# Attention into a SoLU feed-forward layer on one core: a planner that counts TensorE instructions and open transfers, sixteen transposes moved to DMA, constants and first key casts moved off GpSimd

## The chip, the core and the metric

The kernel runs on one core of a Trainium2 chip. The core has five engines, each with an instruction queue of its own: TensorE (PE in the profile, its weight loads PEld), VectorE (DVE), ScalarE (ACT), GpSimd (POOL) and SyncE (SP, which here only issues transfers). Sixteen DMA engines move the data. The metric is the device time of one execution in microseconds (us), lower is better.

## What is computed

Inputs are q, k and v of shape (4 batches, 8 heads, 768 positions, 64), float32, and the feed-forward weights. Each query sees the first 8 positions and the 96 latest ones; a bias grows with the distance. The attention output of all heads is one row of 512 per token (3072 tokens), and each row goes through a SoLU layer with a layer norm and an output product.

```python
scores = scale * np.matmul(q, k.transpose(0, 1, 3, 2)) + bias
scores = np.where(is_global | is_local, scores, -1e9)
a = exp(scores - max); a = a / sum(a)
x = np.matmul(a, v)                      # -> (3072, 512)
h = x @ w_in                             # w_in  512 x 1024
solu = h * softmax(h)
ln = (solu - mean) / sqrt(var + 1e-6) * g_ln
out = ln @ w_out                         # w_out 1024 x 512
```

## The kernel before

The program is built in two passes. First the kernel describes its work as 1,316 steps: each has an engine, a duration in ns, a priority, the steps that it depends on, the buffers that it takes and frees, and a function that records its instructions (`step`, line 146). Then `Plan.order` (line 165) plays the steps through: an engine that is free takes the waiting step of lowest priority number whose buffers are to be had, and the order in which steps start is the order in which their instructions are recorded. Priorities come from the table `PRIO` (line 28), one number for each step, which replaces those written in the code. The instruction order of every queue is therefore fixed when the program is built; on the chip each queue runs it in order and waits on semaphores. Where the planner sees a gap of over 330 ns on TensorE in the first 60 us, it puts in dummy matmuls on `busy16` (line 1187).

The steps, by stage:

- **Constants** (lines 410 to 495): identity matrices, the local bias `bw`, masks and ones, most of them written by GpSimd.
- **Loads**: SyncE issues nearly all (`load`, line 634). q and k of a pair of heads come in one transfer of 384 KB, v in two; for the first 256 positions of batch 0 there are small loads `qnat` and `knat` in the natural layout. The feed-forward weights `w_out` are 4 transfers of 512 KB on SyncE, `w_in` 2 on GpSimd's queue.
- **Per batch and pair of heads**: GpSimd casts q and k to fp16 (line 752), TensorE transposes them (line 765), DVE copies them out of PSUM (lines 775, 777). TensorE adds bias and scores (lines 868, 878), ACT takes the exponential into `eb` (line 886).
- **Per unit of 256 or 384 queries**: scores of the global keys (line 921), sums of the exponentials (lines 946, 953), products with v (lines 1030, 1039); the reciprocal of the sums goes through DRAM (`rd`, `rb`) in batches 1 to 3; DVE multiplies it in and writes `xT` (line 1077).
- **Per token tile** (24 tiles of 128 tokens): TensorE makes h with 8 matmuls of 512 columns (line 1110, here g1), ACT its exponential `ef` (line 1117), DVE the product `uu` (line 1120), ACT the sum of squares (line 1124). TensorE transposes `uu` in 8 pieces (line 1131), DVE copies them to `uT` (line 1135), and 8 more matmuls of 512 columns with the scaled weights `gw_out_sb` give the output (line 1169, here g2). ACT scales it into `osb` (line 1175), and SyncE stores 256 KB (line 1177). The weights `gw_out_sb` are first scaled by ACT (line 680), their mean is taken by 8 matmuls (line 686, here the mean step), and DVE writes the final ones (line 690).

A loaded weight and a matmul are two TensorE instructions, so 8 matmuls are 16 instructions. `uT` has 7 buffers, `uu` 3, `osb` 3. PSUM has 8 banks; g1 takes a pair of them, g2 one, a transposition of `uu` one.

Of the kernel before, what the change touches and what calls it, by code (L numbers as in the profile page):

```python
# [18 lines left out]
P = 128  # L19
# [106 lines left out]
"""  # L126
LDQ = 4


class Plan:  # L130

# [1094 lines left out]
```

## Time and profile before

| | before |
|---|---|
| median of 3 runs | 196.66 us (195.24 to 197.91) |
| the profiled execution | 194.31 us |
| its span from the first to the last instruction | 192.1 us |
| mean granted TensorE clock | 0.952 of full speed |
| bytes moved by DMA | 33.62 MB |

The page of the profile gives the busy time of each engine, the span in 40 slices, the DMA queues, and the chain of waits: the work that ended last, followed back from the end. In the chain "issue" is time in which an engine waited for nothing that the profile shows. The view of waits lists who waited for whom; the view by windows gives for any stretch the busy time of each engine, the number of its instructions and the busy share of the DMA engines; the timeline lists instructions in order of time.

### The profile page before, as it was taken

How to read it: one execution, taken by the hardware profiler on the slowest of the kernel's cores; microseconds unless marked ns; L12 is line 12 of the kernel's file. 1: busy time of each engine (PE TensorE's matmuls, PEld its weight loads, DVE VectorE, ACT ScalarE, POOL GpSimd, SP SyncE). 2: the span in 40 equal slices, each digit the busy share in tenths (PEclk: the TensorE clock that was granted, in tenths of full speed). 3: DMA queues.
4: the chain of work that ended last, by engine and by line, in shares of the span. 5: the costliest groups of instructions: out<-in, count | busy, mean ns of one | idle time of the engine just before them, and what ended most of it. 6: DMA issues, size and time to landing. Idle time of an engine off the chain costs nothing.

```text
span 192.1 us, 5950 instructions
## 1 busy us (share of the span) xinstructions
PE 168.4 (88%) x2456; PEld 98.1 (51%) x2456; DVE 109.6 (57%) x237; ACT 120.4 (63%) x228; POOL 56.9 (30%) x142
## 2 busy tenths in 40 slices
PE   6959779959799979977799999999999289999992
PEld 2434555646355565746445466774656124555550
DVE  1985254855389996544454667774474622555820
ACT  2001967895799865552479993686987002997861
POOL 7889546533260547303513105300000000000000
PEclk9987999996999999997999999999999958999998
DMA  6988985799989297999489997700009900130052
GB/s 142 276 220 158 268 207 125 190 359 372 221 294 307 67 286 224 252 232 306 153 190 195 240 254 214 228 20 0 3 5 218 269 12 0 43 121 3 0 218 109
DMA packets 48363, 33.62 MB, mean 175 GB/s; under 512 B 32417, under 2 KB 43729, under 8 KB 48337
## 3 DMA queue, kind: packets, MB, share of 16 engines
q1 hardware_dynamic: 45536, 31.64, 59.9%
q0 software_dynamic: 544, 1.05, 3.1%
q10 hardware_dynamic: 2256, 0.56, 1.3%
q8 instruction: 19, 0.31, 0.7%
q14 instruction: 8, 0.06, 0.1%
HBM read 27.92 MB, written 6.37 MB: 178 GB/s over the span
## 4 chain that ended last, share of the span: by engine, by line
PE 61%; DVE 11%; issue 11%; ACT 10%; DMA 3%; POOL 1%; ACTq 1%; POOLq 0%; DVEq 0%
PE bank L1169 20%; PE bank L1110 16%; PE bank L1039 5%; PE bank L765 5%; PE bank L1131 4%; ACT ef L1117 3%; ACT eb L886 3%; DVE uu L1120 3%; PE bank L868 2%; DVE gw_out_sb L690 2%; PE bank L878 2%; DMA qnat<-in_q_dram 2%; DVE qT L777 2%; PE bank L1030 2%; DVE uT L1135 2%
## 5 line engine op out<-in xcount | busy, mean ns | idle before, releaser
L1169 PE MATMUL bank<-gw_out_sb,uT 128*128 128x512 f16 x192 | 46.2, 390 | 0.1
L1110 PE MATMUL bank<-w_in_sb,xT 128*128 128x512 f16 x192 | 45.5, 385 | 0.0
L1120 DVE SCALAR_TENSOR_TENSOR uu<-ef,bank 128x1024 f16<-128x1024 f16 x24 | 29.1, 1220 | 28.1 <-ACT ef L1117 28.1
L886 ACT ACTIVATE eb<-bank 128x896 f16<-128x896 f32 (+3 forms) x36 | 29.2, 855 | 21.7 <-PE bank L878 21.5
L1117 ACT ACTIVATE ef<-bank 128x1024 f16<-128x1024 f32 x24 | 24.5, 1021 | 20.2 <-PE bank L1110 20.1
L1169 PEld LDWEIGHTS <-uT 128*128 128x128 f16 x192 | 18.4, 100 | 26.7 <-issue 6.9
L1110 PEld LDWEIGHTS <-xT 128*128 128x128 f16 x192 | 18.2, 100 | 20.8 <-issue 1.6
L1124 ACT ACTIVATE sq<-uu 128x1024 f16<-128x1024 f16 x24 | 25.4, 1059 | 3.5 <-DVE uu L1120 3.0
L1039 PE MATMUL bank<-eb,v 64*64 64x160 f16 (+4 forms) x464 | 18.1, 227 | 9.8 <-issue 9.2
L1175 ACT ACTIVATE osb<-bank,rstd 128x512 f32<-128x512 f32 x24 | 16.0, 683 | 11.2 <-PE bank L1169 9.2
L1135 DVE COPY uT<-bank 128x1024 f16<-128x1024 f16 x24 | 16.2, 687 | 9.5 <-PE bank L1131 7.4
L752 POOL CAST k<-k 128x768 f16<-128x768 f32 (+1 forms) x16 | 12.4, 772 | 24.4 <-PE bank L765 16.5
L777 DVE COPY qT<-bank 128x768 f16<-128x768 f16 (+1 forms) x16 | 14.0, 886 | 6.5 <-PE bank L765 6.5
L827 POOL CAST v<-v 128x704 f16<-128x704 f32 (+2 forms) x24 | 13.3, 577 | 13.7 <-issue 7.6
L1039 PEld LDWEIGHTS <-v 64*64 64x64 f16 x464 | 14.4, 114 | 5.4 <-issue 4.9
L1187 PE MATMUL bank<-busy 128*128 128x512 f16 x44 | 14.8, 476 | 1.5 <-DVE busy L624 1.5
L1077 DVE TENSOR_TENSOR xT<-bank,rb 128x384 f16<-128x384 f32 x24 | 12.2, 552 | 6.8 <-PE bank L1039 5.0
L777 DVE COPY kT<-bank 128x768 f16<-128x768 f16 (+1 forms) x16 | 13.9, 883 | 3.3 <-PE bank L765 3.3
L752 POOL CAST q<-q 128x768 f16<-128x768 f32 (+1 forms) x16 | 12.4, 776 | 10.3 <-DMA q<-in_q_dram 6.4
L1131 PEld LDWEIGHTS <-uu 128*128 128x128 f16 x192 | 12.0, 98 | 4.7 <-DVE uu L1120 1.1
L1131 PE MATMUL bank<-ident,uu 128*128 128x128 f16 x192 | 14.2, 219 | 0.1
L1030 PE MATMUL bank<-eg,vgz 64*64 64x192 f16 (+1 forms) x144 | 12.4, 246 | 2.0 <-issue 2.0
(96 smaller groups left out, 220.2 us busy)
## 6 DMA issues: line engine op xcount, KB each, us to landing
out_dram<-osb SPq DMA_DIRECT2D x24, 256.0 KB
k<-in_k_dram SPq DMA_DIRECT2D x12, 384.0 KB
q<-in_q_dram SPq DMA_DIRECT2D x12, 384.0 KB
rb<-rd SPq DMA_DIRECT2D x12, 384.0 KB
v<-in_v_dram SPq DMA_DIRECT2D x12, 192.0 KB
w_out<-in_moe_w_out_dram SPq DMA_DIRECT2D x4, 512.0 KB
v<-in_v_dram SPq DMA_DIRECT2D x12, 160.0 KB
k<-in_k_dram SPq DMA_DIRECT2D x4, 256.0 KB
```

The lines of the kernel that those rows point to most:

```text
L752: nc.gpsimd.tensor_copy(out=o, in_=a)
L777: nc.vector.tensor_copy(out=d_.rearrange("p (g j) -> p g j", j=run), in_=pt.rearrange("p (j g) -> p g j", j=run))
L886: ex["fn"] = (lambda ex=ex, qk=qk, gw=gw: nc.scalar.activation(out=eb[at(qk, "eb")][:, :, 0:gw], in_=big(qk)[:, :, 0:gw], func=AF.Exp, sca ...
L1030: nc.tensor.matmul(out=o_[64 * h : 64 * h + 64, x * n : x * n + n], lhsT=(onesz[r, 2 * pair + h] if pv is None else vgz[r, b, 2 * pair + h ...
L1039: nc.tensor.matmul(out=o_[64 * h : 64 * h + 64, gl : gl + m], lhsT=onesv[r, :] if pv is None else vv[r, v_at(vi, h, c), pair, :], rhs=view ...
L1110: nc.tensor.matmul(out=ph()[:, ts(fh, 512)], lhsT=xT[at(xt_own[b], "xT")][:, j, ts(t % NA, P)], rhs=w_in_sb[:, j, ts(fh, 512)], start=(j = ...
L1117: ex["fn"] = lambda g1=g1, t=t, ph=ph: nc.scalar.activation(out=ef[at(g1, "ef")], in_=ph(), func=AF.Exp, accum_out=s0[:, t : t + 1])
L1120: u["fn"] = lambda u=u, g1=g1, t=t, ph=ph: nc.vector.scalar_tensor_tensor(out=uu[at(u, "uu")], in0=ef[at(g1, "ef")], scalar=USC, in1=ph(), ...
L1124: sqs["fn"] = lambda u=u, t=t: nc.scalar.activation(out=sq, in_=uu[at(u, "uu")], func=AF.Square, accum_out=s2[:, t : t + 1])
L1131: nc.tensor.transpose(out=pt[:, ts(c, P)], in_=uu[at(u, "uu")][:, ts(c, P)], identity=ident)
L1135: el["fn"] = lambda lt=lt, el=el: nc.vector.tensor_copy(out=uT[at(el, "uT")].rearrange("p c f -> p (c f)"), in_=one(lt).bitcast(FP16))
L1169: nc.tensor.matmul(out=one(g2), lhsT=uT[at(el_x, "uT")][:, c, :], rhs=gw_out_sb[:, c, :], start=(c == 0), stop=(c == NFC - 1))
```

## The change

The planner gets two more things to count. `count` is the number of TensorE instructions of a step: it supposes that instructions come in chunks of 256, that the next chunk is asked for 110 instructions before a chunk's end, and that it arrives some time later, behind the transfers open at that moment; a step that needs a chunk that is not there gets longer. `ring` is the room for open transfers: a load takes some of 140 units when it is issued and gives it back when its transfer is done, and a load that finds no room waits. Some durations of loads are set anew, and the whole table `PRIO` is another, so that the order of every queue changes.

For the 16 tiles from number 8 on (`TURNED`), the transposition of `uu` by TensorE and the copy by DVE are replaced by one transposing DMA on SyncE's queue from `uu` to `uT`. GpSimd's constants are split into smaller steps, and part of them (slopes, key masks, zeros of `kg`, ones) go to DVE. The four casts of `knat` go from GpSimd to ACT.

```diff
+TURNED = set(range(8, 24))
...
+    RING = 140
+    CHUNK, ASK, DRY = 256, 110, 196
+    FETCH, BEHIND, ARRIVE = 1300, 800, 2400
...
-                    if not can(s["take"]):
+                    if s["eng"] != "DMA" and s["ring"] > ring or not can(s["take"]):
...
+                    if s["eng"] == "DMA":
+                        heapq.heappush(events, (now + dur, seq, 3, s["ring"]))
+                        seq += 1
+                    else:
+                        ring -= s["ring"]
...
+                    if s["count"]:
+                        read += 2 * s["warm"][1]
+                        at = read + s["count"]
+                        while self.CHUNK * chunk - self.ASK < at:
+                            ask = self.CHUNK * chunk - self.ASK
+                            t = now + (max(0, ask - read) * dur) // s["count"]
+                            coming.append((self.CHUNK * chunk + self.DRY, self.ARRIVE + max(
+                                t + self.FETCH, drained + self.BEHIND)))
+                            chunk += 1
+                        while coming and coming[0][0] < at:
+                            dry, t = coming.pop(0)
+                            t0 = now + (max(0, dry - read) * s["dur"]) // s["count"]
+                            dur = max(dur, s["dur"] + t - t0)
+                        read = at
...
+    def constants_slopes():
...
-                nc.gpsimd.memset(sl[hf, p : p + 1], -slopes[2 * p + h] / inv_sqrt_d / BSC)
+                nc.vector.memset(sl[hf, p : p + 1], -slopes[2 * p + h] / inv_sqrt_d / BSC)
...
-    id_st = step("POOL", 1086, -90000, [], constants_ident)
-    iota_st = step("POOL", 2238, -89000, [], constants_iota)
-    pick_st = step("POOL", 2490, -88000, [], constants_pick)
-    sums_st = step("POOL", 1007, -50000, [], constants_sums)
+    id_st = step("POOL", 560, -90000, [], lambda: constants_ident(ident, 1.0))
+    idb_st = step("POOL", 560, -88500, [], lambda: constants_ident(identb, BSC))
+    iota_st = step("POOL", 460, -89000, [], constants_iota)
+    iotag_st = step("POOL", 900, -88000, [], constants_iota_g)
+    pick_st = step("POOL", 1200, -88000, [], constants_pick)
+    slope_st = step("DVE", 620, -89000, [], constants_slopes)
+    keys_st = step("DVE", 1250, -70500, [], constants_keys)
+    sums_st = step("DVE", 500, -50000, [], constants_sums)
...
-    def load(fn, us, prio, deps, eng="SP", take=(), iss=500, bulk=False):
+    def load(fn, us, prio, deps, eng="SP", take=(), iss=500, bulk=False, ring=256):
...
+                on_act = natural and nm == "k"
...
-                    nc.gpsimd.tensor_copy(out=o, in_=a)
+                    if on_act:
+                        nc.scalar.activation(out=o, in_=a, func=AF.Copy)
+                    else:
+                        nc.gpsimd.tensor_copy(out=o, in_=a)
...
-        lt = step("PE", 460, tt + 4500, [u, id_st], None, take="one", mode="f")
...
+        if t in TURNED:
+            el, lt = load(lambda s, u=u: nc.sync.dma_start_transpose(
+                out=uT[at(s, "uT")], in_=uu[at(u, "uu")]),
+                1300, tt + 4500, [u], take=("uT",), iss=1700)
+            ready_u = lt
+        else:
+            lt = step("PE", 460, tt + 4500, [u, id_st], None, take="one", mode="f", mm=8)
...
         plan.release(u, "uu", [sqs, lt])
```

More of the change, by code (lines that the diff above doesn't have):

```diff
@@ L184, in order @@
         done = 0
+        ring = self.RING
+        drained = 0
+        read = 0
+        chunk = 1
+        coming = []
         def can(take):
@@ L687, in mean @@
                                  start=(j == 0), stop=(j == NFC - 1))
-        wm = step("PE", 1790, 25000, wr + [sums_st, hold], mean, mode="f")
+        wm = step("PE", 1790, 25000, wr + [sums_st, hold], mean, mode="f", mm=8)
         w_st = [step("DVE", 740, 30000 + 100 * j, [wm], lambda j=j:
@@ L741, in do_part, with cast @@
                     need = [dma]
-                cs = step("POOL", 394 if natural else 20 + 1.01 * n, t0 - 1200, need, None,
+                on_act = natural and nm == "k"
+                cs = step("ACT" if on_act else "POOL",
+                          400 if natural else 20 + 1.01 * n, t0 - 1200,
+                          need + [table_st] * on_act, None,
                           take=nm + "16_", free=[(iss, nm + "32_")] if iss else [])
-                def cast(cs=cs, iss=iss, x32=x32, x16=x16, nm=nm, run=run, natural=natural, p=p):
+                def cast(cs=cs, iss=iss, x32=x32, x16=x16, nm=nm, run=run, natural=natural, p=p,
+                         on_act=on_act):
                     o = x16[at(cs, nm + "16_")][:, 0:run].rearrange("p j (h d) -> p j h d", h=2)
@@ L755, in do_part @@
                 tps = step("PE", run * 57, t0, [cs, id_st], None,
-                           take=("one", dn) if new else "one", free=[cs], mode="f")
+                           take=("one", dn) if new else "one", free=[cs], mode="f",
+                           mm=run)
                 if new:
@@ L785, in do_part @@
                     new_g = p == 0
-                    kc = step("POOL", 215, t0 + 1000, [ev, pick_st] + ([] if new_g else [kg_own[b]]),
+                    kc = step("POOL", 215, t0 + 1000, [ev, keys_st] + ([] if new_g else [kg_own[b]]),
                               None, take=("kg",) if new_g else ())
@@ L907 @@
             gs = step("PE", 4 * hw_ * 0.43 + 50, tS - 2000,
-                      kg_st[b] + [x for p in range(NPR) for x in q_ready[p][: ui + 1]] + [far_st, id_st],
-                      None, take=("one", "eg"), mode="s")
+                      kg_st[b] + [x for p in range(NPR) for x in q_ready[p][: ui + 1]] + [far_st, idb_st],
+                      None, take=("one", "eg"), mode="s", mm=9)
             for p in range(NPR):
@@ L974 @@
                         256 * (12 + 0.28 * w / 1.0) / 16, tS + 4000, [dd] + ([bi] if bi else []),
-                        take=() if bi else ("rb",), iss=600)
+                        take=() if bi else ("rb",), iss=650)
                     bi = bi or s_
@@ L1098 @@
         tt = T0 + TT * t
-        g1 = step("PE", 1790, tt, xt_st[t] + w_in_st, None, take=("big", "ef"), mode="f")
+        g1 = step("PE", 1790, tt, xt_st[t] + w_in_st, None, take=("big", "ef"), mode="f", mm=8)
         g1_of.setdefault(b, []).append(g1)
@@ L1125, with pet @@
             out=sq, in_=uu[at(u, "uu")], func=AF.Square, accum_out=s2[:, t : t + 1])
-        lt = step("PE", 460, tt + 4500, [u, id_st], None, take="one", mode="f")
-        def pet(lt=lt, u=u):
-            pt = one(lt).bitcast(FP16)
-            for c in range(NFC):
-                nc.tensor.transpose(out=pt[:, ts(c, P)], in_=uu[at(u, "uu")][:, ts(c, P)],
-                                    identity=ident)
-        lt["fn"] = pet
-        el = step("DVE", 700, tt + 5000, [lt], None, take="uT", free=[lt])
-        el["fn"] = lambda lt=lt, el=el: nc.vector.tensor_copy(
-            out=uT[at(el, "uT")].rearrange("p c f -> p (c f)"), in_=one(lt).bitcast(FP16))
-        chain[t] = (u, sqs, el)
+        if t in TURNED:
[5 more added lines that the diff above has]
+            lt = step("PE", 460, tt + 4500, [u, id_st], None, take="one", mode="f", mm=8)
+            def pet(lt=lt, u=u):
+                pt = one(lt).bitcast(FP16)
+                for c in range(NFC):
+                    nc.tensor.transpose(out=pt[:, ts(c, P)], in_=uu[at(u, "uu")][:, ts(c, P)],
+                                        identity=ident)
+            lt["fn"] = pet
+            el = step("DVE", 700, tt + 5000, [lt], None, take="uT", free=[lt])
+            el["fn"] = lambda lt=lt, el=el: nc.vector.tensor_copy(
+                out=uT[at(el, "uT")].rearrange("p c f -> p (c f)"), in_=one(lt).bitcast(FP16))
+            ready_u = el
+        chain[t] = (u, sqs, el, ready_u)
         plan.release(u, "uu", [sqs, lt])
@@ L1163 @@
                 tg = tt + 6500 + TT * (x - grp[0])
-                g2 = step("PE", 1790, tg, [el_x] + w_st, None, take="one", free=[el_x],
-                          mode="f")
+                g2 = step("PE", 1790, tg, [chain[x][3]] + w_st, None, take="one", free=[(el_x, "uT")],
+                          mode="f", mm=8)
                 def pe2(el_x=el_x, g2=g2):
```

83 lines of the change are left out of this document (48 added, 35 removed), and 192 rows, old and new, of the table PRIO.

## The prediction, made before the changed kernel ran

> **What bounds the kernel now.** I read the page first, then the chain of waits, then windows around the gaps that the chain shows on TensorE.
>
> ```profile
> span 192.1 us, 5950 instructions
> ...
> PE 168.4 (88%) x2456; PEld 98.1 (51%) x2456; DVE 109.6 (57%) x237; ACT 120.4 (63%) x228; POOL 56.9 (30%) x142
> ...
> PE 61%; DVE 11%; issue 11%; ACT 10%; DMA 3%; POOL 1%; ACTq 1%; POOLq 0%; DVEq 0%
> ```
>
> ```profile
> q8 instruction: 19, 0.31, 0.7%
> ```
>
> TensorE is busiest and carries 61% of the chain. The odd entry is "issue", 11%: time in which the engine waited for nothing that the profile shows. The chain in order of time has six large pieces of it:
>
> ```profile
> 23.03 1.96 issue
> ...
> 41.22 1.84 issue
> ...
> 47.61 1.65 issue
> ...
> 85.06 2.65 issue
> ...
> 92.36 1.27 issue
> ...
> 149.95 4.69 issue
> ...
> 154.90 3.53 PE bank L1169 x8
> 158.42 2.60 PE bank L1110 x8
> ...
> 180.52 1.73 PE bank L1169 x8
> 182.25 0.89 PE bank L1131 x16
> ```
>
> They sum to 14.06 us. The windows say what they are. Each row runs from the start to one of the gaps; its counts are the matmuls and weight loads until then:
>
> ```profile
> 0.00:23.50 23.50, 19.27 (x223) 9.93 (x224) 12.97 (x36) 6.16 (x10) 18.82 (x78) 0.93 0.89 213
> 0.00:41.50 41.50, 34.95 (x607) 20.27 (x608) 23.71 (x64) 20.46 (x43) 28.93 (x96) 0.96 0.84 210
> 0.00:47.70 47.70, 39.50 (x735) 23.64 (x736) 26.98 (x73) 24.21 (x52) 30.45 (x100) 0.93 0.87 231
> 0.00:85.50 85.50, 74.16 (x1247) 44.57 (x1248) 54.92 (x120) 53.09 (x102) 45.04 (x123) 0.96 0.86 233
> 0.00:92.50 92.50, 78.81 (x1375) 48.37 (x1376) 58.30 (x128) 54.96 (x105) 46.80 (x126) 0.94 0.88 239
> 0.00:150.50 150.50, 134.68 (x2271) 81.88 (x2272) 92.34 (x199) 98.56 (x185) 56.91 (x142) 0.97 0.77 201
> ```
>
> PE plus PEld is 447, 1215, 1471, 2495, 2751 and 4543: every time a multiple of 256 plus 191. So TensorE runs dry at fixed places of its own instruction stream, and the page's queue q8 with 19 instruction transfers of 0.31 MB (16 KB, 256 instructions of 64 bytes) is what it waits for. There are 18 such places, and six hurt. Which ones, the 151 matmuls ahead of a place tell:
>
> ```profile
> 79.19:84.83 5.64, 5.64 (x153) 3.98 (x151) 4.55 (x7) 4.05 (x6) 0.94 (x2) 1.00 1.02 229
> 123.86:127.13 3.27, 3.26 (x166) 2.75 (x154) 2.45 (x8) 3.27 (x5) 0.00 (x0) 1.00 0.30 103
> 146.94:149.73 2.79, 2.79 (x151) 2.69 (x151) 1.54 (x6) 1.11 (x3) 0.00 (x0) 1.00 1.06 212
> ```
>
> With the DMA engines full (the column before the last, 1.02 and 1.06) a lead of 5.64 us ends in the 2.65 us gap and one of 2.79 us in the 4.69 us gap, so the block comes some 7.5 to 8.3 us after that point; at a share of 0.30 a lead of 3.27 us leaves no gap. The longest gap costs more than itself: the 16 matmuls behind it take 6.13 us (3.53 + 2.60) where 16 take 3.46 later (1.73 for 8), 2.67 us.
>
> The Trainium skill has a rule against this reading ("Runtime: NRT & Kernel Launch", Instruction fetch mechanics): blocks of 16 KiB are prefetched and crossing one is "mostly hidden". The block size agrees with q8; the hiding does not hold here, where six of 18 places show gaps.
>
> **The change, term by term**, against the profiled execution: 194.31 us, of which 192.1 is the span.
>
> *Sixteen tiles turned by DMA: gain on TensorE.* 128 matmuls and their weight loads go: 8 take 0.445 us (0.89 for 16), so 16 x 0.445 = 7.1 us. In the late stage TensorE never pauses (27.00 us busy in the row from 161 us below), so all of it is on the path. The 16 DVE copies that go as well were beside TensorE's work. They count as nothing.
>
> *The gaps.* The mean step parts the ramp from the rest:
>
> ```profile
> 55.21 1.89 PE L686 MATMUL bank<-gw_out_sb,onesm 128*128 128x512 f16 x8
> ```
>
> After it the old kernel loses 2.65 + 1.27 + 4.69 + 2.67 = 11.28 us. For the new order I tallied the 151 matmuls ahead of each place, with 1.73 us for 8 large ones, 0.056 for a transposition, and for the small ones these rows:
>
> ```profile
> 119.61 0.67 PE bank L765 x12
> ...
> 122.66 0.21 PE bank L878 x12
> 123.12 0.21 PE bank L868 x4
> ```
>
> ```profile
> 147.66 0.08 PE bank L1030 x4
> ...
> 148.07 0.14 PE bank L1039 x12
> ```
>
> Late in the new order the shortest leads are at the thirteenth and fourteenth place, both about 4.9 us (the thirteenth: 48 score matmuls 0.84, 12 bias 0.63, 12 transpositions 0.67, 8 large 1.73, 55 products with v 0.64, 16 global ones 0.32); all others after the mean step are over 7. At 4.9 us a place costs nothing at a light DMA load and 8.2 - 4.9 = 3.3 at a full one; I take 1.5 for each, 3.0 in all (0 to 6.6). Before the mean step the new leads are no better: about 3.1, 3.4 and 3.5 us at the fourth to sixth place, where the old ones lost 1.96 + 1.84 + 1.65 = 5.45. There I give no gain. Net: -11.3 + 3.0.
>
> *The start.* The first exponentials wait 14 us at the end of GpSimd's chain of constants and casts, two of whose rows are:
>
> ```profile
> 10.65 0.20 POOL L412 MEMSET ident<- 128x128 f16 x1
> ...
> 18.48 0.39 POOL L752 CAST k<-knat 128x256 f16<-128x256 f32 x1
> ```
>
> ```profile
> 18.58 2.48 ACT L886 ACTIVATE eb<-bank 128x576 f16<-128x576 f32 x4 [14.14 <-PE bank L878]
> ```
>
> ```profile
> 4.05 3.81 DMA qnat<-in_q_dram
> ```
>
> The first query loads land at about 8 us (4.05 + 3.81 for the third). In the new order the identity stands ahead of the casts, which could then begin with the data: the first exponential may come 8 us earlier. The four casts (0.39 each) fall into ACT's 14.14 us; if that cover is gone by then, they cost 1.6. DVE gets 29 small memsets, some 3.0 us at GpSimd's price of 0.10, and has 3.43 us in which it waits for GpSimd's `ti`; without that cover the bias and so the first scores come 3 us later:
>
> ```profile
> L427 POOL MEMSET sl<- 64x1 f32 x8 | 0.8, 102 | 0.3
> ```
>
> ```profile
> 4.89 0.24 DVE L430 CAST gw_out_sb<-ti 128x160 f32<-128x160 int32 x1 [3.43 <-POOL ti L420]
> ```
>
> But the ramp also waits for transfers. The weights `w_out` stand behind 10.33 MB of SyncE's transfers now and behind 9.15 before; at the 231 GB/s of the window to 47.70 us that is 5.1 us later for the mean step, which both orders reach with the same TensorE work behind them (25.6 and 25.7 us by the same rows). So from -8 to +5; I take -3, nearer to the gain, since the share of 0.87 leaves room.
>
> *What the transposing DMA costs.* No row shows one. The nearest is the store of the same 256 KB:
>
> ```profile
> L1177 SPq DMA_DIRECT2D out_dram<-osb x24: 332/344/2754, 65.6 to 189.1; - x24
> ```
>
> ```profile
> SPq L1221 <- DMA out_dram<-osb: 1.4, 1, 1.4
> ```
>
> Its issue holds SyncE 0.34 us (2.75 when the queue is full), and the last one, with the queue empty, lands some 2 us after its issue began (0.34 + 1.4 and the steps between). The far end is the query load above, 3.81 us for 128 KB, so 7.6. I take 4, nearer to the store of the same size. The wait that is new is SyncE's for `uu`; behind it stand stores, the reciprocals' round trip and the last v and q loads. SyncE is mostly idle by then, so a held queue costs at most single issues. In the new order the second product of a turned tile comes at the tightest 7.2 us of TensorE work after its first one, and for the last two tiles 8.6 us. The exponential and `uu` stand between:
>
> ```profile
> L1120 DVE SCALAR_TENSOR_TENSOR uu<-ef,bank 128x1024 f16<-128x1024 f16 x24 | 29.1, 1220 | 28.1 <-ACT ef L1117 28.1
> ...
> L1117 ACT ACTIVATE ef<-bank 128x1024 f16<-128x1024 f32 x24 | 24.5, 1021 | 20.2 <-PE bank L1110 20.1
> ```
>
> They take 1.02 and 1.22 us, with the hand-overs some 3.0, which leaves 4.2 and 5.6: at 4 us it is hidden, at 7.6 it costs 3.4 there and 2.0 at the end. In the last stage ACT is the next to be late:
>
> ```profile
> 161.00:188.00 27.00, 27.00 (x169) 13.89 (x166) 14.38 (x33) 21.14 (x42) 0.00 (x0) 1.00 0.18 69
> ```
>
> ACT is busy 21.14 of 27.00 us. Without the seven transpositions in it (3.1 us) it would be 21.14 of 23.9, still below. For both I put +1.5.
>
> Dummy matmuls are 46 against 44: nothing.
>
> **The sum.** 194.3 - 7.1 - 11.3 + 3.0 - 3.0 + 1.5 = 177.4 for a profiled execution. The profiled one lies 2.35 us below the median of the runs shown (196.66), so about 180 for the median. With each term at its ends this case reaches from 171 to 186.
>
> **Rivals.**
> - *The gaps stay after the mean step.* If the two leads of 4.9 us fall into full DMA, with one clock loss of 2.67 and some more at leads of 7 to 8, nothing of the 8.3 net is won: 188. If the rule of hiding held and the gaps were something else, it would be the same: the change would not do what it says. The counts speak against that.
> - *The ramp waits for transfers*, +5 in place of -3: 188. For it speaks a DMA share of 0.87 up to 47.70 us. With the first rival 196, no change.
> - *ACT becomes the bound of the last stage*: its share goes to 0.88 there, and an order in which it waits once per tile loses perhaps 5 us: 185.
> - *Transposing DMAs pass one after the other, too slowly*: slower. Between the first products of the last twelve tiles and the last second product lie 41.8 us of TensorE work (11 tiles x 2 x 1.73, and 3.8 of other steps); less 3.0 for the lead that is 3.2 us for each tile. At a price p above 3.2 the end moves by 12 x (p - 3.2): from p = 4.9 on the kernel is over 2% slower, at 7.6 it takes 233. For it speaks that no transfer here does such work; against it that the store of as many bytes is through in about 2 us, and others may be under way beside it. The Trainium skill ("VectorE: DVE Perf Modes", The three transpose paths) gives 1309 ns for one 128x128 block by DMA against 390 on TensorE; eight in series would be an estimated 10.5 us a tile, and 12 x (10.5 - 3.2) = 88 us on top. Against that figure for TensorE the trace has 56 ns a block when they follow each other.
>
> **Chances.** Forecast 0.48; gaps stay 0.17; ramp 0.15; both of these 0.06; ACT 0.05; slow transposes 0.09. Two per cent, about what a measurement of this kernel can tell from no change, is 192.7 to 200.6. So faster is 0.48 + 0.17 + 0.15 + 0.05 = 0.85, the same 0.06, slower 0.09. The range 171 to 191 leaves out the slow transposes, the joint case, and a little below.
>
> **What would show it.** Gaps of "issue" on TensorE after 60 us under 4 us in sum, and still at 256 k + 191; in the ramp three of them near 3 us of lead. First exponential near 10 us. Second products that hardly wait for a DMA of `uT`; from SyncE's issue to landing about 4 us. The mean step between 47 and 60 us tells the ramp. It is wrong if TensorE waits for `uT` tile after tile in the last 50 us, if ACT has no idle time there, or if the gaps sum to over 10 us after the mean step.

## The result, and the profile after

| | before | after |
|---|---|---|
| median | 195.95 us (194.48 to 197.91, 4 runs) | 181.89 us (180.28 to 185.88, 4 runs) |
| ratio after / before | | 0.929 (95% interval 0.920 to 0.939) |
| profiled execution | 194.31 us, span 192.1 | 185.88 us, span 184.0; a second one 182.96 us, span 181.1 |
| mean step begins | 55.21 us | 61.41 us; 61.15 in the second |
| from there to TensorE's last matmul | 133.1 us | 118.8 us; 116.2 in the second |

The change made the kernel 7.1% faster: 14.1 us. The first profile of the changed kernel is of a disturbed execution (185.88 us, 4 us over the median), so a second one stands beside it where stages are timed. The last two rows hold the story. The mean step parts the kernel into a ramp, up to it, and the rest. In these two profiles the ramp is 6 us longer than in the one before, and the rest 14 to 17 us shorter.

From the page of the first profile after:

```profile
span 184.0 us, 5709 instructions
...
PE 160.2 (87%) x2330; PEld 90.5 (49%) x2330; DVE 103.0 (56%) x250; ACT 121.3 (66%) x232; POOL 53.2 (29%) x109
...
DMA packets 65258, 37.80 MB, mean 205 GB/s; under 512 B 49312, under 2 KB 60624, under 8 KB 65232
...
PE 53%; DMA 16%; DVE 14%; issue 6%; SPq 5%; ACT 3%; POOL 2%; DVEq 0%; POOLq 0%; ACTq 0%
```

TensorE is still the busiest engine, with 2,330 matmuls where it had 2,456: 128 transpositions fewer and two dummies more. "Issue" falls from 11% of the chain to 6%, DMA rises from 3% to 16%. The chain in order of time says where each of them sits (start, length, what; the longest pieces of the ramp, the mean step, and all of "issue" over 0.4 us behind it):

```profile
29.41 3.34 DMA k<-in_k_dram
...
33.58 6.49 DMA k<-in_k_dram
...
45.81 2.53 issue
...
53.00 2.08 issue
...
61.43 2.67 PE bank L733 x8
...
94.94 0.44 issue
...
104.09 0.46 issue
```

Before the mean step (L733) the chain now runs through two loads of k, 9.8 us, which the chain before did not have, and two gaps at 256k+191 remain. Behind it, where the old kernel had 2.65, 1.27 and 4.69 us, one gap of that kind is left, of 0.21 us at 133.04; the two later pieces of "issue" lie on DVE and ACT. Most of the DMA in this chain is not k: `rb<-rd`, the reciprocals on their way back from DRAM, takes 10.6% of the span. Waiting for it, `xT` is late twice, and TensorE waits 1.6 and 1.3 us for `xT`; in the second profile it does not.

The last stage and the new transfers, in the window of the last 25 us and in the view of the tile `uT` (duration of the issue as min/median/max; then who waited; then the time from issue to landing):

```profile
155.00:180.20 25.20, 25.20 (x117) 11.27 (x115) 10.37 (x25) 18.84 (x37) 0.00 (x0) 1.00 0.85 183
```

```profile
L1184 SPq DMA_TRANSPOSE uT<-uu x16: 1231/1256/4010, 91.4 to 172.4; - x16
...
  PEld L1233: 1.6, 2
  PE bank L1233: 1.1, 1
...
DMA to landing us min/median/max: 3.8/4.8/5.4
```

TensorE does not pause in the last 25.20 us, and ACT is busy 18.84 of them: it did not become the bound. The sixteen transposing DMAs land 3.8 to 5.4 us after their issue (3.3 to 6.3 in the second profile), and TensorE's second products waited once for one, 1.1 us (0.4 in the second).

### The profile page after: what moved, and what is told of

The parts are those of the page before. It is cut to its first block, busy times and chain, and to the rows that moved or that the text cites. A ratio compares the mean times of both kernels' runs of the same rounds, so it can differ in the third digit from the quotient of the medians.

```text
span 184.0 us, 5709 instructions
## 1 busy us (share of the span) xinstructions
PE 160.2 (87%) x2330; PEld 90.5 (49%) x2330; DVE 103.0 (56%) x250; ACT 121.3 (66%) x232; POOL 53.2 (29%) x109
## 2 busy tenths in 40 slices
DMA packets 65258, 37.80 MB, mean 205 GB/s; under 512 B 49312, under 2 KB 60624, under 8 KB 65232
## 4 chain that ended last, share of the span: by engine, by line
PE 53%; DMA 16%; DVE 14%; issue 6%; SPq 5%; ACT 3%; POOL 2%; DVEq 0%; POOLq 0%; ACTq 0%
PE bank L1167 15%; PE bank L1233 14%; DMA rb<-rd 11%; DMA k<-in_k_dram 5%; PE bank L1096 5%; PE bank L820 4%; PE bank L1251 4%; PE bank L924 3%; PE bank L934 2%; DVE gw_out_sb L737 2%; PE bank L977 2%; PE bank L1087 2%; DVE uu L1177 2%; SPq L648 2%; PE bank L733 1%
## 5 line engine op out<-in xcount | busy, mean ns | idle before, releaser
L1167 PE MATMUL bank<-w_in_sb,xT 128*128 128x512 f16 x192 | 44.4, 379 | 1.1 <-DVE uu L1177 1.0
L1233 PE MATMUL bank<-gw_out_sb,uT 128*128 128x512 f16 x192 | 44.3, 379 | 1.1 <-DMA uT<-uu 1.1
L1096 PE MATMUL bank<-eb,v 64*64 64x160 f16 (+4 forms) x464 | 17.3, 223 | 2.7 <-issue 2.1
L806 POOL CAST k<-k 128x768 f16<-128x768 f32 (+1 forms) x16 | 12.3, 774 | 24.9 <-DMA k<-in_k_dram 14.5
L832 DVE COPY kT<-bank 128x768 f16<-128x768 f16 (+1 forms) x16 | 13.9, 887 | 9.5 <-PE bank L820 9.5
L1251 PE MATMUL bank<-busy 128*128 128x512 f16 x46 | 15.7, 481 | 1.7 <-DVE busy L670 1.5
L924 PE MATMUL bank<-bw,identb 64*64 64x448 f16 (+3 forms) x144 | 13.8, 364 | 1.4 <-DVE xT L1134 1.3
L934 PE MATMUL bank<-qT,kT 64*64 64x160 f16 (+4 forms) x416 | 13.8, 229 | 0.2 <-issue 0.2
L820 PE MATMUL bank<-ident,q 128*128 128x128 f16 x96 | 9.3, 232 | 5.0 <-POOL q L806 3.0
```

Of the source, the lines that this page charges most:

```text
L806: nc.gpsimd.tensor_copy(out=o, in_=a)
L832: nc.vector.tensor_copy(out=d_.rearrange("p (g j) -> p g j", j=run), in_=pt.rearrange("p (j g) -> p g j", j=run))
L924: nc.tensor.matmul(out=sc[o : o + 64, par, 0:gw], lhsT=identb[r, r], rhs=bw[r, p, a0 : a0 + gw], start=True, stop=False, tile_position=(64 ...
L934: nc.tensor.matmul(out=sc[o : o + 64, par, col : col + n], lhsT=kk[r, BLK * c : BLK * c + BLK], rhs=qq[r, g0 : g0 + n], start=False, stop= ...
L1096: nc.tensor.matmul(out=o_[64 * h : 64 * h + 64, gl : gl + m], lhsT=onesv[r, :] if pv is None else vv[r, v_at(vi, h, c), pair, :], rhs=view ...
L1167: nc.tensor.matmul(out=ph()[:, ts(fh, 512)], lhsT=xT[at(xt_own[b], "xT")][:, j, ts(t % NA, P)], rhs=w_in_sb[:, j, ts(fh, 512)], start=(j = ...
```

## The experiments

Twelve variants. Each keeps the order of all queues but for what its edit says. Times are medians; those of the changed kernel were 181.89 and 182.01 us in two comparisons, of the kernel before 195.25 to 197.30.

### The changed kernel again

No edit.

> The changed kernel unaltered, for a second profile to stand beside those of the variants. Theory (the ramp was stretched by transfers, the part behind the mean step did what was forecast): the mean step again begins some 4 to 6 us later than the 55.21 us of the kernel before, and from it to the end of TensorE's work it takes 117 to 120 us against 133 before; no gap of over 0.5 us at 256k+191 instructions behind the mean step. Rival (the late mean step of the first profile came from its low clock alone): the mean step begins within 1.5 us of 55.2.

Measured: 182.01 us, ratio to before 0.927 (0.916 to 0.939). The mean step:

```profile
L733 PE MATMUL bank<-gw_out_sb,onesm x8: 379/379/390, 61.1 to 62.7; 128*128 128x512 f16 x8
```

The mean step is late again, at 61.15 us, at a mean clock of 0.981 of full speed, so the lost clock of the first profile isn't the cause. Behind it lie 116.2 us, just under the 117 to 120 expected, and one gap at 256k+191, 1.14 us at 129 us, more than the 0.5 expected. In two other variants that change nothing ahead of the mean step (the added transpositions below) it began at 57.80 and 59.41 us: the ramp varies, and is 2.6 to 6.2 us longer in four profiles than in the one profile before. The old ramp varies too: in the variant of the old kernel below that leaves it as it is (the transposing DMA alone) the mean step began at 57.24 us, 2.0 later than before. So the ramp is longer, but by how much is known only to within several microseconds.

### Do the gaps belong to the instruction stream?

Two edits shift the stream and do nothing else. To the changed kernel 64 small matmuls (128 instructions, half a block) are added where TensorE waits for its first data:

```diff
+    extra = 64
     for s in plan.order():
...
+        if count and extra:
+            for _ in range(extra):
+                nc.tensor.matmul(out=bank[spot // 2][:, spot % 2, 0:64], lhsT=busy16[:, 0:P],
+                                 rhs=busy16[:, 0:64], start=True, stop=True)
+            extra = 0
```

> The changed kernel with 64 small matmuls (128x64, on data that nothing reads) put once behind the first dummy matmuls, where TensorE waits for the first query casts anyway; every queue keeps its order. So each piece of work stands 128 TensorE instructions later in the stream, half a block. Theory (gaps come from the fetch of 256-instruction blocks, and the new order has its long leads only at its own places): by the leads in the changed kernel's trace, gaps come back behind the mean step at about 84, 105 and 130 us, about 2.9, 4.1 and 2.3 us, together 7 to 10, and the kernel takes 6 to 10 us longer than the changed one. Rival (the gaps were waits of something else, which the new order removed): no new gaps, within 1 us of the changed kernel.

Measured: 189.50 us, ratio to before 0.969 (0.959 to 0.980), 7.5 more than the changed kernel. TensorE's waits from 62 us on (who waited for what: us in all, times, longest), and a window to the first of them:

```profile
PE bank L1194 <- issue: 5.4, 1, 5.4
PE bank L934 <- issue: 1.8, 1, 1.8
```

```profile
0.00:84.00 84.00, 68.15 (x1247) 42.29 (x1248) 50.46 (x144) 50.09 (x101) 38.13 (x83) 0.94 0.88 222
```

The long gap, 5.44 us up to 85.55, stands behind 1247 + 1248 = 2495 instructions, 9 x 256 + 191. The sum of the two gaps, 7.2 us, was expected (7 to 10), and their places near 85 and 133 us; the one near 105, expected at 4.1 us, did not come. The transfer of the instruction queue for that place was over at 106.18 us, 1.6 us before TensorE reached it; why it came so early is open.

The same to the kernel before, with 24 small matmuls (48 instructions):

> The kernel before with 24 such small matmuls behind its first dummies, so that all work stands 48 instructions later; no other difference. Theory (fetch): the gaps of 2.65 us near 85 us and of 4.69 us near 150 us go, one of about 3.4 us near 92 us takes the place of the 1.27 us, a small one of about 1.2 near 127; behind the mean step about 4.6 us in place of 8.6, and without the lost clock the kernel is 4 to 7 us faster than before. Rival (something else): same time and the six gaps stand before the same work as they did.

Measured: 188.63 us, ratio to before 0.965 (0.954 to 0.975): 6.6 us faster by 24 useless matmuls. TensorE's waits from 57 us to the end in the kernel before, and from 60 us on in the variant:

```profile
PE bank L1039 <- issue: 7.3, 2, 4.7
PE bank L946 <- issue: 1.3, 1, 1.3
PE bank L921 <- DVE uT L1135: 1.0, 1, 1.0
PE bank L1039 <- DVE xT L1077: 0.4, 1, 0.4
```

```profile
PE bank L1039 <- DVE xT L1077: 1.8, 2, 1.5
PE bank L921 <- DVE xT L1077: 1.6, 1, 1.6
PE bank L921 <- DVE uT L1135: 1.0, 1, 1.0
PE bank L1169 <- DVE xT L1077: 0.2, 1, 0.2
```

All of TensorE's "issue" is gone behind the mean step; what is left are waits put down to DVE, of which one of 1.5 us sits at the place of a block (2,751 instructions). The mean step itself began at 58.5 us, 3.3 later than before, so the gain lies behind it. The work and its order are the same in both. So the gaps belong to places in the instruction stream and not to the work that stands there, in both directions.

That the thing waited for is the instructions themselves can be read from the times of the transfers on q8. In the kernel before, blocks of 16 KB move from 85.05 to 86.38 us and from 152.23 to 153.31, and TensorE goes on 1.3 us behind each end, at 87.71 and 154.63, out of the gaps of 2.65 and 4.69 us. So it is at all 19 gaps of over 0.1 us at 256k+191 in five profiles (before, changed twice, these two variants): the gaps last 0.15 to 5.44 us, and TensorE always goes on 1.25 to 1.63 us after a block has landed. The wait of 1.5 us at 2,751 instructions is one of them, so one gap is left in the old kernel with 24 matmuls, where 3.4 us were expected. The prediction's first reading is shown. The Trainium skill ("Runtime: NRT & Kernel Launch", Instruction fetch mechanics) says that the crossing of a 16 KiB block is mostly hidden; these runs disagree by 7.5 and 6.6 us.

### What are 128 transpositions on TensorE worth?

To the changed kernel 8, then 16 transpositions of constant data are added ahead of each second product of a turned tile, into the bank that it overwrites:

```diff
-                def pe2(el_x=el_x, g2=g2):
+                def pe2(el_x=el_x, g2=g2, x=x):
+                    for c in range(NFC):
+                        if x in TURNED:
+                            nc.tensor.transpose(out=one(g2).bitcast(FP16)[:, ts(c, P)],
+                                                in_=busy16[:, 0:P], identity=ident)
```

> The changed kernel with 8 transpositions of constant data by TensorE ahead of the second product of each of the 16 turned tiles, into the bank that this product then overwrites; the transposing DMAs stay. It gives TensorE back the instructions that the change took away. Theory (all of this time is on the path): 16 x 0.445 = 7.1 us longer than the changed kernel, and up to 1 us more by a fetch place that moves to a shorter lead; 6.5 to 8.5 in all. Rival (TensorE has slack in the late stages, since it waits for the transposing DMAs): under 3 us longer.

> The changed kernel with 16 transpositions of constant data ahead of each of the 16 second products, twice as many as in the variant that cost 4.5 us (186.49 against 182.01). By the leads the losses at fetch places behind the mean step change by less than 1 us. Theory A (the changed kernel has some 2.6 us of slack behind the mean step, in waits that the first eight used up; the rest is on the path): 4.5 + 7.1 = 11.6 us above 182.0, so 193 to 194.5. Theory B (eight of them cost less than 0.445 us in this place): 9.0, so 190 to 192. Theory C (7.1 is right, and the 4.5 was a ramp that happened to be short in those runs): 14.2, so 195 to 197; then the time from the mean step to TensorE's end, 123.5 us in the profile of the first variant, goes to 130.5.

Measured: 186.49 us (ratio 0.955, 0.945 to 0.964) and 192.44 us (0.987, 0.981 to 0.993), so 4.5 us for the first 128 and 5.95 for the next. In the trace eight of them take 0.45 us, as expected, 7.2 for 128 and 14.3 for 256. So 4.5 of 7.2 and 10.4 of 14.3 appear in the time. In the medians theory C (all of it) and the first rival (nearly none) both miss; A and B lie 1.2 and 1.4 us from what was measured, and stay undecided. By the profiles the stage behind the mean step grows from 116.2 to 123.5 and 127.6 us, 7.3 and 4.1 more: all of the first 128 is on the path there, and in that profile a ramp 3.4 us shorter, which the edit does not touch, hides part of it in the time. What hides a part of the second 128 is not known. What the 16 copies on DVE were worth, which went with the transpositions, no run tests.

### The transposing DMA alone, in the old order

```diff
-        lt["fn"] = pet
+        lt["fn"] = pet if t < 8 else None
...
+        if t >= 8:
+            el["fn"] = lambda u=u, el=el: nc.sync.dma_start_transpose(
+                out=uT[at(el, "uT")], in_=uu[at(u, "uu")])
```

> The kernel before with the transposing DMA alone: for tiles 8 to 23 the 8 transpositions on TensorE go and the copy on DVE is replaced, at its place in the recorded order, by the transposing DMA; no other queue changes. Theory (TensorE's time is on the path and the DMA is hidden): 7.1 us less work; the fetch places move by 16 instructions per tile, by the leads in the old trace the gap near 150 us goes (4.69 and 2.67 of lost clock) and one of about 1 comes near 125; against that the second products stand only 3.1 to 8.7 us behind their tile's product, so that a landing 3.8 to 5.4 us after the issue makes some of them wait, about 3 us in all. Sum: 8 to 12 us faster than before. Rival (the waits for the DMA take the gain back): within 3 us of the kernel before.

Measured: 204.75 us, ratio to before 1.051 (1.042 to 1.059), where 8 to 12 us less were expected. The waits of the engines from 60 us on and of SyncE's queue (SPq) from 60 to 200 us, then the landing:

```profile
PE bank L1172 <- DMA uT<-uu: 18.9, 8, 4.2
DVE uu L1120 <- DMA uT<-uu: 11.8, 4, 4.1
```

```profile
SPq L1180 <- ACT osb L1178: 27.4, 9, 8.0
```

```profile
DMA to landing us min/median/max: 3.0/3.1/3.8
```

The DMA lands as soon as expected, 3.0 to 3.8 us after its issue. But its issue stands in SyncE's queue behind stores (L1180) that wait for ACT: 12 of the 16 are issued 1.7 to 8.4 us after the product that they turn, where in the changed kernel 14 of 16 are issued within 1.5 us of it. The second product then waits, 18.9 us in eight times; and as the DMA has not yet read `uu`, DVE waits 11.8 us for one of its three buffers. And the stores wait for ACT's `osb`, which waits 24.9 us for second products, so each late issue makes the next one later. Both theories thought of the landing, and the wait ahead of the issue cost more.

The same for the first eight tiles, in the new order, with the 64 small matmuls so that later fetch places stay:

```diff
-            lt["fn"] = pet
...
-            el["fn"] = lambda lt=lt, el=el: nc.vector.tensor_copy(
-                out=uT[at(el, "uT")].rearrange("p c f -> p (c f)"), in_=one(lt).bitcast(FP16))
+            el["fn"] = lambda u=u, el=el: nc.sync.dma_start_transpose(
+                out=uT[at(el, "uT")], in_=uu[at(u, "uu")])
```

> The changed kernel with the transposing DMA for the first eight tiles too, at the place of DVE's copy in the order, and the 64 small matmuls of the earlier variant at the start, so that from the ninth tile on every fetch place is where it is in the changed kernel. 64 transpositions fewer on TensorE: 8 x 0.445 = 3.6 us; six of the eight tiles lie behind the mean step. Their second products stand 7.4 us or more behind their tile's product, the DMA lands 3 to 6 us after its issue. Theory (TensorE's time behind the mean step is on the path): 2 to 4 us less than the changed kernel, so 178 to 180. Rival (a landing under a full DMA load is too late for the two tiles with 7.4 and 7.8 us, or SyncE held by a wait for the product delays the loads behind it): within 1 us or longer.

Measured: 206.95 us, ratio to before 1.070 (1.057 to 1.083), 25 us over the changed kernel. TensorE's longest wait behind the ramp (us in all, times, longest), SyncE's timeline (start, length), and DVE's:

```profile
PE bank L1227 <- DMA uT<-uu: 22.0, 3, 11.8
```

```profile
80.24 4.20 SPq L1192 DMA_TRANSPOSE uT<-uu  x1
84.49 0.58 SPq L586 DMA_DIRECT2D k<-in_k_dram  x1
85.11 1.37 SPq L586 DMA_DIRECT2D q<-in_q_dram  x1
86.58 9.56 SPq L1235 DMA_DIRECT2D out_dram<-osb  x3
96.32 1.53 SPq L1192 DMA_TRANSPOSE uT<-uu  x1
```

```profile
74.17 1.22 DVE L1177 SCALAR_TENSOR_TENSOR uu<-ef,bank 128x1024 f16<-128x1024 f16 x1 [0.24 <-ACT ef L1174]
75.31 0.08 DVE L1177 DVE_READ_ACCUMULATOR uu<-ef,bank 128x1 f32 x1
75.31 1.22 DVE L1177 SCALAR_TENSOR_TENSOR uu<-ef,bank 128x1024 f16<-128x1024 f16 x1
...
91.25 1.22 DVE L1177 SCALAR_TENSOR_TENSOR uu<-ef,bank 128x1024 f16<-128x1024 f16 x1 [12.44 <-DMA uT<-uu]
```

The products of three tiles were done by 76.5 us; the first of their transposing DMAs is issued at 80.24 and the next at 96.32, in the places that the order gave to DVE's copies. The fourth `uu` waits 12.44 us, and three second products 22.0, nearly all of the 25. The step, not its engine, has to be moved: in the changed kernel the issue stands near its product in SyncE's queue.

### Where the ramp lost its time

Three edits that were to find it did not. First GpSimd's relief, undone (the same in the key masks, the sums and the ones):

```diff
-                nc.vector.memset(sl[hf, p : p + 1], -slopes[2 * p + h] / inv_sqrt_d / BSC)
+                nc.gpsimd.memset(sl[hf, p : p + 1], -slopes[2 * p + h] / inv_sqrt_d / BSC)
...
-                    if on_act:
-                        nc.scalar.activation(out=o, in_=a, func=AF.Copy)
-                    else:
-                        nc.gpsimd.tensor_copy(out=o, in_=a)
+                    nc.gpsimd.tensor_copy(out=o, in_=a)
```

> The changed kernel with the constants that went to DVE (slopes, key masks, zeros of kg, ones) and the four first key casts recorded on GpSimd again, at their places in the order; nothing else is moved. Theory (what ends the start is the landing of the first keys, so the relief of GpSimd was worth nothing): first scores and time within 1 us of the changed kernel. Rival, the forecast's own term (the chain on GpSimd sets the first exponential): 3 us longer, 8 at most.

Measured: 182.41 us, 0.4 more. TensorE's bias ahead of the first scores came 3 to 4 us later (21.4 us against 17.2 and 18.1), the mean step 1.2 us later (62.6), the end not measurably. So GpSimd did set the first scores by then, against the theory, and they do not set the time by the 3 us or more of the forecast's term; less than the ramp varies by would not be seen.

Second, the four loads of the first keys (`knat_iss` holds their issues) at the front of SyncE's queue:

```diff
-    for s in plan.order():
+    seq = plan.order()
+    first = [s for s in seq if any(s is x for x in knat_iss)]
+    for s in first + [s for s in seq if not any(s is x for x in knat_iss)]:
```

> The changed kernel with its four loads of the first keys moved to the front of SyncE's queue; all else keeps its order. Theory (the first scores wait for the third and fourth of these loads, issued at 7.6 and 10.3 us): the first casts of keys come near 9 us and the first scores at 12 to 14 in place of 17 to 18. Whether the whole gets faster tells the second thing: if the rest of the ramp waits for later transfers, which come no sooner, the mean step and the time stay within 1.5 us; if the start itself was on the path, 3 to 5 us less.

Measured: 183.33 us, ratio to before 0.935 (0.923 to 0.946), no gain, and not because a gain was swallowed later: the first scores, by the same mark, came at 19.3 us, no earlier. The v load behind them now landed later, GpSimd waited 3.1 us for it with the next q casts behind, and the first key casts started at 16.0. It shows that several loads of the start are late together, and leaves open what an earlier start would be worth.

Third, three of the four loads of `w_out` left out, and DVE's final weights read the same two chunks as ACT's:

```diff
-        w_out_st = [load(lambda i, j=j: nc.sync.dma_start(
+        w_out_st = [load(lambda i, j=j: j or nc.sync.dma_start(
...
-                               out=gw_out_sb[:, j, :], in_=w_out32[:, j, :], func=AF.Copy,
+                               out=gw_out_sb[:, j, :], in_=w_out32[:, j % 2, :], func=AF.Copy,
```

> The changed kernel with one of the four loads of w_out: the scaling and the final weights of all eight chunks read the first two chunks, so the second product is made with other weights than the reference's, by the same instructions. 1.5 MB less stand in SyncE's queue at about 42 to 44 us. Theory (the ramp is bound by transfers): loads behind them land up to 1.5 MB / 231 GB/s = 6.5 us sooner; the mean step comes 2 to 6 us earlier and the time falls by 2 to 6. Rival (the ramp is bound by the order on TensorE and by the two fetch gaps): mean step and time within 1 us.

Measured: 181.01 us, 1.0 less, the mean step at 61.3. So the mean step does not wait for `w_out`; TensorE's waits for casts of q and k stay, 5.3 us between 24 and 62 us. What it stands behind is the attention of the next batch, and here the two orders differ. GpSimd's casts of k and q from 20 to 48 us (duration min/median/max, first and last start), before and then after in the second profile:

```profile
L752 POOL CAST k<-k x4: 609/722/827, 30.4 to 43.9; 128x512 f16<-128x512 f32 x2, 128x768 f16<-128x768 f32 x2
L752 POOL CAST q<-q x4: 612/720/827, 22.9 to 39.1; 128x768 f16<-128x768 f32 x2, 128x512 f16<-128x512 f32 x2
```

```profile
L806 POOL CAST k<-k x7: 609/617/827, 23.5 to 46.8; 128x512 f16<-128x512 f32 x4, 128x768 f16<-128x768 f32 x3
L806 POOL CAST q<-q x7: 609/825/827, 22.7 to 47.5; 128x768 f16<-128x768 f32 x4, 128x512 f16<-128x512 f32 x3
```

Fourteen against eight: the new order wants q and k earlier, and not many more of them, since up to each one's mean step it is 18 casts against 15, and 19 loads of q and k are issued in both. The DMA engines do not move more in that time (columns: length, busy time of PE, PEld, DVE, ACT, POOL, clock, DMA share, GB/s), each to its mean step:

```profile
0.00:55.20 55.20, 45.36 (x801) 26.83 (x802) 30.83 (x80) 30.58 (x64) 33.34 (x105) 0.94 0.88 231
```

```profile
0.00:61.10 61.10, 46.87 (x878) 28.28 (x878) 35.69 (x107) 32.97 (x68) 31.88 (x76) 0.94 0.87 226
```

231 GB/s over 55.2 us is 12.8 MB, 226 over 61.1 is 13.8: 1.0 MB more, 4.6 us at that rate. By itself this proves nothing, since at an equal rate any longer ramp moves more. The test is to halve the bytes of the q and k loads, in both kernels; each head pair then computes with the q and k of its first head:

```diff
-            out=dst[:, 0 : 2 * run * D].rearrange("g (h x) -> g h x", h=2),
+            out=dst[:, 0 : run * D],
             in_=bass.AP(tensor=rows.tensor, offset=rows.offset + lo * D,
-                        ap=[[run * D, P], [S * D, 2], [1, run * D]]))
+                        ap=[[run * D, P], [1, run * D]]))
...
-                        a = x32[at(iss, nm + "32_")][:, 0 : 2 * run * D].rearrange(
-                            "p (h j d) -> p j h d", h=2, j=run)
+                        a = x32[at(iss, nm + "32_")]
+                        a = bass.AP(tensor=a.tensor, offset=a.offset,
+                                    ap=[a.ap[0], [D, run], [0, 2], [1, D]])
```

> The changed kernel with half the bytes in every load of q and k but the first 256 positions of batch 0: of each pair of heads only the first is loaded, and the cast reads it for both, so that head pairs compute with one head's q and k. Instructions of the engines are the same. By about 55 us some 2.4 MB less are moved. Theory (the ramp of the new order waits for transfers of q and k, which it asks for earlier than the old one): the waits of TensorE for GpSimd's casts of q and k go (3.9 to 5.3 us in the profiles), the two gaps at 256k+191 shrink, and the mean step comes at 52 to 57 us in place of 61; time 4 to 9 us less than the changed kernel's 182. Rival (engine work and order bind the ramp, transfers only accompany it): the mean step within 1.5 us of 61.

> The same halving of the q and k loads in the kernel before. Theory (its order asks for fewer q and k before the mean step, so it waits less for them): besides the gaps at 256k+191, which shrink with the load on the DMA engines, the mean step comes at most 2 to 3 us earlier than 55.21, clearly less than in the changed kernel. Rival (both ramps hang on transfers alike): the same gain in both.

Measured: 177.04 us for the changed kernel so altered, 5.0 less, with a ratio to before of 0.917 (0.896 to 0.937); for the kernel before 193.81 us and a ratio of 0.998 (0.988 to 1.009), no difference. The mean step, changed kernel first:

```profile
L733 PE MATMUL bank<-gw_out_sb,onesm x8: 379/379/389, 56.4 to 58.0; 128*128 128x512 f16 x8
```

```profile
L686 PE MATMUL bank<-gw_out_sb,onesm x8: 376/378/379, 55.2 to 56.7; 128*128 128x512 f16 x8
```

Against the second profile the new ramp shrinks by 4.7 us, to 1.2 above the old length; the old one begins its mean step where it did. TensorE's 3.9 us of waits for casts of q and k between 24 and 62 us are gone, one of the two remaining fetch gaps too. These were the waits, in the second profile:

```profile
PE bank L820 <- POOL k L806: 2.3, 3, 1.0
...
PE bank L820 <- POOL q L806: 1.6, 2, 0.9
```

The four profiles of the unaltered new ramp have 1.5 to 3.9 us of them, and a load of k of 6.46 to 7.27 us in each chain; the two of the old ramp have 0 and 0.6 us, and no load of k in the chain, but one of them a load of q, 3.4 us. So the new ramp waits for transfers of q and k, and the old one hardly did. How many of the microseconds lost that explains is less sure: 56.4 us is only 1.4 ahead of the earliest unaltered mean step (57.80), and the interval of the ratio overlaps that of the changed kernel (0.916 to 0.939).

No variant that loads all its data was faster than the changed kernel.

## Why the prediction was right, and where it was not

The forecast was 180 us with a range of 171 to 191; measured 181.9. The direction and most of the size came from the right reasons, the gaps and the transpositions. That the number came within 2 us is partly luck: two of its terms were off by several microseconds each and partly made up for one another.

| term | forecast | shown |
|---|---|---|
| 128 transpositions off TensorE | -7.1 | 7.2 us of work; put back, 4.5 us in the median and 7.3 behind the mean step; for as many again 5.95 and 4.1 |
| gaps and clock behind the mean step | -11.3 + 3.0 | -11.3 + 0.2 in the first profile, + 1.1 in the second |
| start and ramp | -3.0 | mean step 2.6 to 6.2 us later in four profiles |
| transposing DMA and ACT | +1.5 | 1.1 us of TensorE's waits in the first profile, 0.4 in the second; ACT not the bound |

- **The gaps** were read rightly: fixed places of TensorE's stream, and a new order that has longer leads there. The two leads of 4.9 us were sized too short. They were tallied from work alone; in the first profile after they are 7.0 and 6.6 us, and 1.5 and 1.3 of it are waits (for the transposing DMA and GpSimd, and for DVE): a lead that contains a wait is longer by that wait. In the second profile no wait stands ahead of the fourteenth place, and there the gap of 1.14 us came. Of the 3.0 put in for the two places, 0.2 and 1.1 came.
- **The transpositions**: the row gave the right price. "All of it is on the path" holds behind the mean step for the first 128 put back (7.3 us), not for as many again (4.1); in the medians two thirds to three quarters return.
- **The DMA's price** of 4 us from issue to landing, taken between 2 and 7.6, met 4.8 (3.8 to 5.4) and 5.1 (3.3 to 6.3) in the second profile, and it was nearly hidden, as forecast. The queue that it holds was put at single issues; in the first profile one return of the reciprocals was issued behind a store and a transposing DMA, and TensorE lost 1.3 us to it, in the second none. But the prediction weighed only the landing against the 7.2 us of lead. The two variants that turn tiles in places chosen for a copy show the price that was missing: the wait for the issue in SyncE's queue, and DVE's wait for `uu`. They ended 9.4 and 25 us slower. The prediction's rival on the slow side had the right transfer and the wrong reason, a serial engine; the DMAs do not pass one by one, for by its rule 4.8 us a tile would have given some 199 us; an issue behind other waits is late. Of the Trainium skill's 1309 ns a block ("VectorE: DVE Perf Modes", The three transpose paths) eight in series would be an estimated 10.5 us; the landing of 3.8 to 5.4 us is below that.
- **The start** is the step that failed. "I take -3, nearer to the gain, since the share of 0.87 leaves room": the share is a mean over 47.7 us, and the end that was priced beside it, 5.1 us for 1.2 MB more ahead of `w_out`, is nearer to what came. The first exponential, forecast 8 us earlier, came at 18.85 us (17.91 in the second profile) against 18.58. The price was put on the wrong transfers, though: `w_out` is not waited for, the q and k loads of the next batch are. This is the second rival, given 0.15, in its kind and near it in size (+5 against 2.6 to 6.2). Its 188 is 185.4 for a profiled execution, and the two took 185.88 and 182.96; the part behind the mean step came out up to 3 us better than the sum's (14.3 and 16.9 us against 13.9).
- **Ramp gaps**: no gain was given there; 5.45 us became 4.61 in the first profile and 3.1 in the second.

The sum for a profiled execution was 177.4, and the two profiled ones took 182.96 and 185.88; the median was forecast with 2.35 on top, as the profile before lay below its median. The two profiles after lie above theirs, and this, too, brought the forecast nearer to the measured median: luck. The range has a slip: with every term at its worse end (6.6 for the gaps, +5 for the ramp, 1.5) the sum ends near 191 and not 186; the range as stated, 171 to 191, about covers it. What would have shown the steps wrong was named: the mean step was to lie between 47 and 60 us and lay at 61, and the first exponential near 10. Both say that the start's term did not come.

## What to carry to other kernels

Where an engine idles for nothing that the profile shows, count its instructions up to each gap: if the remainder is the same each time, suspect instruction fetch; a few useless instructions ahead of it are a cheap test and here were a cure for the old order. Before a step is moved to a DMA, look for its place in the issuing queue and for the buffers that it holds until it lands, not only for its price. Where an order changes, compare when each order asks for its transfers, not the mean share of the DMA engines.

## What the hardware did that was not expected

- TensorE stands still until a block of its instructions has landed, and 1.25 to 1.63 us more, at 19 gaps in five profiles. Twenty-four matmuls without use made the old kernel 6.6 us faster, and sixty-four made the new one 7.5 us slower, by moving the places at which TensorE waits for its instructions.
- A transposing DMA of 256 KB is moved in small pieces: the page counts 65,258 packets after, 48,363 before. In the last stage the DMA share is 0.85, where the old last stage had 0.18.
- Its issue holds SyncE's queue 1.26 us in the median, 4.0 at most, where the store of as many bytes held it 0.34.
